# A six-layer cross network on one core: how the last layer's third round is evicted, and where the pending sum stands

## The chip, the core and the metric

The kernel runs on one core of a Trainium2 chip. The metric is the device time of one execution in microseconds (us), as the median of several runs; lower is better. The engines are named as the profile names them: PE is the matrix engine (PEld its weight loads), DVE the vector engine, ACT the scalar engine, POOL GpSimd, and SP the engine whose queue issues most DMAs here. A "q" behind a name (SPq, ACTq) is that engine's instruction queue.

## What is computed

x0 has 4096 rows of 416 numbers, ws six matrices of 416 by 416, bs six rows of 416; all in bf16.

```python
def reference(x0, ws, bs):
    x = x0
    for l in range(ws.shape[0]):
        x = x0 * (x @ ws[l] + bs[l]) + x
    return x
```

## The kernel before

**Layers 0 to 4** work on the transposed state: features lie on the partitions (three groups of 128 features in `XM`, the last 32 features packed for four column groups in `XR`), and the 4096 rows of the batch lie along the free dimension. PE multiplies with the layer's weights, ACT adds the bias while it copies the result out of PSUM to bf16 (L159), DVE multiplies by x0 (L160) and adds the old state (L161). While layer 4 ends, DMA transposes write its result back with rows on the partitions (`XLrows`, L197), since the output needs rows.

**The last layer** (from L292) exchanges the operands, so that its result has rows on the partitions: a block is 128 rows by 416 outputs. There are 32 blocks, worked off in four rounds of eight. A round covers two "quads" of four blocks. Per round four PSUM tiles are allocated, each with two banks, so that each of the eight blocks has a bank. The pool `psum` has four such tiles, so a tile of a round can be written only when the tile that held its place in the round before has been read by ACT. Which block has which bank is written in the lists `PAIRS`, `TURNS` and `ENDS` (L336 to L338): in `PAIRS` blocks 1 and 2 share a tile, then 3 and 4, and so on; in the other two lists neighbours mostly have different tiles.

PE's order in a round is that of the code at L348 to L354. First come the full products of the first `done` blocks (three matmuls of 128 by 416 each, L304), then for the first quad four matmuls with the last 32 features (L310) and four that add the bias by a row of ones (L313), then the same eight for the second quad, and then the full products of the remaining blocks, each of which closes its block. The last round has `done` = 1, the others 2. A step of PE is in order: a matmul that waits for its tile holds up all behind it.

**Eviction.** `close(u, n)` (L344) calls `ew` (L324) for n neighbouring blocks in one tile, one or two. `ew` lets ACT cast the block or pair from PSUM to bf16 (`t`, L331), DVE multiply it by x0 (`X0rows`, L332), and then calls `close_sum`, which issues what is pending from the block or pair before: DVE's sum with `XLrows` into `o` (L321) and the DMA of `o` to the output (L322). Then its own sum is put into `pending`. So DVE's order is product, sum of the one before, next product, and so on, and `keep_in_program_order` keeps this order. A sum is thus never directly behind its own product. The output DMAs are issued from SP's queue, that of the very last block from ACT's queue. The pool of `t` has 6 buffers, that of `o` has 10.

In the first two rounds blocks are evicted in pairs. In the third round the first two blocks are a pair and the other six are single; in the fourth all eight are single.

Of the kernel before, what the change touches and what calls it, by code (L numbers as in the profile page):

```python
# [16 lines left out]
def kernel(  # L17
# [7 lines left out]
    nc = tc.nc  # L25
    B, D = x0.shape
# [232 lines left out]
    for l in range(1, LL):  # L259
        nxt, nxtR = XM[1 + (l % 2)], XR[1 + (l % 2)]  # L260
        feeds_last = (l == LL - 1)
        tiles = [(s, m) for s in range(NS) for m in range(NK)]
# [31 lines left out]
    NQ = len(quads)  # L294
# [7 lines left out]
    def mm_q_full(q, g, py, closes):  # L302
        for k in range(NK):
            nc.tensor.matmul(py[:, 0:D], lhsT=cur[:, k, q_cols(q, g)], rhs=WM[:, l, k, :],  # L304
                             start=((not closes) and k == 0), stop=(closes and k == NK - 1))

    def mm_q_rem(q, py, done):
        s, i = quads[q]
        for g in range(NG):
            nc.tensor.matmul(py[g][:, 0:D], lhsT=curR[32 * g:32 * g + 32, CW * s + 128 * i:CW * s + 128 * i + 128],  # L310
                             rhs=WR[32 * g:32 * g + 32, l, :], start=(g >= done), stop=False, tile_position=(32 * g, 0))
        for g in range(NG):
            nc.tensor.matmul(py[g][:, 0:D], lhsT=ones[32 * g:32 * g + 1, :],  # L313
                             rhs=bLr[32 * g:32 * g + 1, :], start=False, stop=(g < done), tile_position=(32 * g, 0))
# [3 lines left out]
    def close_sum():  # L318
        while pending:
            o, t, xl, dst, eng = pending.pop()  # L320
            tc.keep_in_program_order(nc.vector.tensor_tensor(out=o, in0=t, in1=xl, op=ALU.add))  # L321
            eng.dma_start(dst, o)  # L322

    def ew(q, g0, n, src, eng):  # L324
        s, i = quads[q]
        b0 = 16 * s + 4 * g0 + i
        b = slice(b0, b0 + 4 * (n - 1) + 1, 4)
        t = tpool.tile([P, 2 * CW], BF16, name="t")
        o = opool.tile([P, 2, D], BF16, name="o")
        tv = t[:, 0:n * D].rearrange("p (a d) -> p a d", a=n)  # L330
        nc.scalar.copy(tv, src)  # L331
        tc.keep_in_program_order(nc.vector.tensor_tensor(out=tv, in0=tv, in1=X0rows[:, b, :], op=ALU.mult))  # L332
        close_sum()
        pending.append((o[:, 0:n, :], tv, XLrows[:, b, :], out_v[:, b, :], eng))

    PAIRS = [(0, 0), (0, 1), (1, 0), (1, 1), (2, 0), (2, 1), (3, 0), (3, 1)]  # L336
    TURNS = [(0, 0), (0, 1), (1, 0), (2, 0), (3, 0), (1, 1), (2, 1), (3, 1)]
    ENDS = [(0, 0), (1, 0), (2, 0), (0, 1), (3, 0), (1, 1), (2, 1), (3, 1)]  # L338
    rounds = [(0, PAIRS, 2), (2, PAIRS, 2), (4, TURNS, 2), (6, ENDS, 1)]
    for q, at, done in rounds:  # L340
        tiles = [psum.tile([P, 2, CW], FP32, tag="ps", name=f"py{n}") for n in range(4)]
        bank = [tiles[n][:, a, :] for n, a in at]

        def close(u, n):  # L344
            tl, a = at[u]
            ew(q + u // 4, u % 4, n, tiles[tl][:, a:a + n, 0:D], nc.scalar if q + 2 == NQ and u == 7 else nc.sync)

        for u in range(done):  # L348
            mm_q_full(q, u, bank[u], False)
        mm_q_rem(q, bank[0:4], done)  # L350
        close(0, done)
        mm_q_rem(q + 1, bank[4:8], 0)
        for u in range(done, 8):
            mm_q_full(q + u // 4, u % 4, bank[u], True)  # L354
            if at is not PAIRS:
                close(u, 1)
            elif u % 2:
                close(u - 1, 2)
# [31 lines left out]
```

## Time and profile before

| | us |
|---|---|
| median of 3 runs | 131.48 (131.47 to 131.52) |
| the profiled execution | 131.97 |
| its span, first to last instruction | 130.1 |
| PE busy | 124.2 (95%) |
| DVE busy | 107.5 (83%) |
| ACT busy | 85.8 (66%) |
| last layer's first full matmul starts | 104.84 |
| last full matmul ends | 125.6 |
| last cast ends | 126.14 |
| last sum starts | 127.01 |
| last output DMA issued (ACT's queue) | 127.42 |

The granted clock of PE was 0.999 over the span. The busy time of an engine counts the time in which at least one of its instructions runs. DVE instructions overlap: the next one starts before the one before it is shown as ended, so what an instruction costs on a busy DVE is the step from its start to the next start, not its duration. The end of a matmul is modelled. A timeline line gives the start, the duration, engine, line of the code, operation, output and inputs, the shapes, and how many were merged; in brackets stands how long the engine had been idle before it and what ended that. The chain of work that ended last, by engine, is PE 89%, DVE 6%, issue 2%, ACT 1%.

### The profile page before, as it was taken

How to read it: one execution, taken by the hardware profiler on the slowest of the kernel's cores; microseconds unless marked ns; L12 is line 12 of the kernel's file. 1: busy time of each engine (PE TensorE's matmuls, PEld its weight loads, DVE VectorE, ACT ScalarE, POOL GpSimd, SP SyncE). 2: the span in 40 equal slices, each digit the busy share in tenths (PEclk: the TensorE clock that was granted, in tenths of full speed). 3: DMA queues.
4: the chain of work that ended last, by engine and by line, in shares of the span. 5: the costliest groups of instructions: out<-in, count | busy, mean ns of one | idle time of the engine just before them, and what ended most of it. 6: DMA issues, size and time to landing. Idle time of an engine off the chain costs nothing.

```text
span 130.1 us, 3968 instructions
## 1 busy us (share of the span) xinstructions
PE 124.2 (95%) x1688; PEld 55.2 (42%) x1690; DVE 107.5 (83%) x197; ACT 85.8 (66%) x97; POOL 5.8 (4%) x17
## 2 busy tenths in 40 slices
PE   6999999999999999999999999999999999999960
PEld 2343343444444444545444434444445445445420
DVE  1012989999998898999898989898989899898991
ACT  0044594788849485849486849577848896569670
POOL 4002110610000000000000000000000000000000
PEclk9999999999999999999999999999999999999999
DMA  3999999999990000000000000000197999995754
GB/s 102 211 219 225 149 198 242 243 327 333 333 306 12 5 0 3 5 0 5 0 5 0 5 0 5 0 0 5 30 176 162 121 220 180 195 306 191 234 170 132
DMA packets 42185, 16.45 MB, mean 126 GB/s; under 512 B 30894, under 2 KB 42168, under 8 KB 42168
## 3 DMA queue, kind: packets, MB, share of 16 engines
q1 hardware_dynamic: 39368, 15.53, 54.4%
q10 hardware_dynamic: 2800, 0.67, 2.8%
q8 instruction: 13, 0.21, 0.7%
q14 instruction: 4, 0.03, 0.1%
HBM read 6.23 MB, written 3.41 MB: 74 GB/s over the span
## 4 chain that ended last, share of the span: by engine, by line
PE 89%; DVE 6%; issue 2%; ACT 1%; DVEq 0%
PE pt L173 49%; PE ph L208 13%; PE py L304 8%; PE pt L179 5%; PE pr L190 5%; DVE t L332 3%; PE wps L135 3%; DVE o L321 2%; PE pr L185 2%; PE ph L226 2%; PE py L310 1%; PE py L313 1%; ACT t L331 1%; PE tpr L151 0%; PE pr L151 0%
## 5 line engine op out<-in xcount | busy, mean ns | idle before, releaser
L173 PE MATMUL pt<-XM,WM 128*32 128x512 bf16 x1152 | 65.2, 379 | 0.0
L159 ACT ACTIVATE t<-pt,bM 128x1024 bf16<-128x1024 f32 x48 | 49.6, 1115 | 17.6 <-PE pt L179 17.6
L160 DVE TENSOR_TENSOR t<-t,XM 128x1024 bf16<-128x1024 bf16 x60 | 41.3, 690 | 6.0 <-ACT t L159 6.0
L161 DVE TENSOR_TENSOR XM<-t,XM 128x1024 bf16<-128x1024 bf16 x60 | 41.7, 696 | 3.4
L173 PEld LDWEIGHTS <-WM 128*32 128x32 bf16 x1152 | 29.8, 97 | 33.9 <-issue 5.4
L331 ACT CAST t<-py 128x416 bf16<-128x416 f32 (+1 forms) x23 | 14.8, 642 | 4.8 <-PE py L304 2.6
L304 PE MATMUL py<-WM,XM 128*128 128x416 bf16 x96 | 17.7, 340 | 0.0
L159 ACT ACTIVATE t<-ph,bM 128x1024 bf16<-128x1024 f32 x12 | 12.5, 1112 | 7.5 <-PE ph L226 7.5
L208 PE MATMUL ph<-XM,WM 128*128 128x512 bf16 x70 | 16.9, 387 | 0.2
L304 PEld LDWEIGHTS <-XM 128*128 128x128 bf16 x96 | 9.0, 98 | 8.5 <-issue 1.4
L332 DVE TENSOR_TENSOR t<-t,X0rows 128x416 bf16<-128x416 bf16 (+1 forms) x23 | 10.4, 456 | 1.2 <-ACT t L331 1.2
L208 PEld LDWEIGHTS <-WM 128*128 128x128 bf16 x72 | 6.9, 99 | 8.9 <-issue 1.9
L321 DVE TENSOR_TENSOR o<-t,XLrows 128x416 bf16<-128x416 bf16 (+1 forms) x23 | 10.4, 455 | 0.0
L165 ACT ACTIVATE t<-pr,bR 128x512 bf16<-128x512 f32 x10 | 6.4, 685 | 3.0 <-PE pr L190 2.1
L190 PE MATMUL pr<-XM,WM 128*32 128x512 bf16 x120 | 8.2, 379 | 0.0
L179 PE MATMUL pt<-XR,WR 32*128 32x512 bf16 x96 | 7.3, 379 | 0.0
L106 ACT ACT_TABLE_LOAD x1 | 1.3, 1283 | 6.6 <-DMA XM<-in_x_dram 6.6
L135 PE MATMUL wps<-warm 128*128 128x512 bf16 (+1 forms) x11 | 4.4, 593 | 1.2 <-DVE warm L94 1.2
L167 DVE TENSOR_TENSOR XR<-t,XR 128x512 bf16<-128x512 bf16 x10 | 4.2, 425 | 0.7
L190 PEld LDWEIGHTS <-WM 128*32 128x32 bf16 x120 | 3.2, 97 | 3.0
L166 DVE TENSOR_TENSOR t<-t,XR 128x512 bf16<-128x512 bf16 x10 | 4.2, 418 | 0.0
L125 POOL COPY WD<-WR 32x32 bf16<-32x32 bf16 (+1 forms) x8 | 3.4, 424 | 16.6 <-DMA WR<-in_ws_dram 16.3
(37 smaller groups left out, 29.7 us busy)
## 6 DMA issues: line engine op xcount, KB each, us to landing
X0rows<-in_x_dram SPq DMA_DIRECT2D x4, 832.0 KB, 11.6
out_dram<-o SPq DMA_DIRECT2D x9, 208.0 KB, 2.5
WM<-in_ws_dram SPq DMA_DIRECT2D x5, 312.0 KB
out_dram<-o SPq DMA_DIRECT2D x13, 104.0 KB, 1.8
WR<-in_ws_dram SPq DMA_DIRECT2D x4, 130.0 KB, 4.1
WM<-in_ws_dram ACTq DMA_DIRECT2D x1, 312.0 KB
XM<-in_x_dram SPq DMA_TRANSPOSE x8, 5.8
xrig<-in_x_dram ACTq DMA_DIRECT2D x4, 32.0 KB, 4.5
```

Of the source, the lines that this page charges most:

```text
L135: nc.tensor.matmul(wps[:, 0:cols], lhsT=warm[:, 0:P], rhs=warm[:, 0:cols], start=True, stop=True)
L159: nc.scalar.activation(t[:], pt[:].rearrange("p a b -> p (a b)"), ACT.Identity, bias=bM[:, m, l:l + 1], scale=1.0)
L160: nc.vector.tensor_tensor(out=t[:], in0=t[:], in1=XM[0][:, m, c0:c0 + 2 * CW], op=ALU.mult)
L161: nc.vector.tensor_tensor(out=nxt[:, m, c0:c0 + 2 * CW], in0=t[:], in1=cur[:, m, c0:c0 + 2 * CW], op=ALU.add)
L173: nc.tensor.matmul(pts[g // 2][32 * q:32 * q + 32, g % 2, :], lhsT=WM[:, l, k, 128 * m + 32 * q:128 * m + 32 * q + 32], rhs=cur[:, k, c0:c ...
L179: nc.tensor.matmul(pts[g // 2][:, g % 2, :], lhsT=WR[32 * g:32 * g + 32, l, 128 * m:128 * m + 128], rhs=curR[32 * g:32 * g + 32, CW * s:CW ...
L190: nc.tensor.matmul(pr[32 * g:32 * g + 32, :], lhsT=WM[:, l, k, NK * P:D], rhs=cur[:, k, c0:c0 + CW], start=False, stop=(k == NK - 1), tile ...
L208: nc.tensor.matmul(pt[m][:, gl, :], lhsT=WM[:, 0, k, 128 * m:128 * m + 128], rhs=cur[:, k, c0:c0 + CW], start=(k == 0), stop=False)
L304: nc.tensor.matmul(py[:, 0:D], lhsT=cur[:, k, q_cols(q, g)], rhs=WM[:, l, k, :], start=((not closes) and k == 0), stop=(closes and k == NK ...
L321: tc.keep_in_program_order(nc.vector.tensor_tensor(out=o, in0=t, in1=xl, op=ALU.add))
L331: nc.scalar.copy(tv, src)
L332: tc.keep_in_program_order(nc.vector.tensor_tensor(out=tv, in0=tv, in1=X0rows[:, b, :], op=ALU.mult))
```

## The change

The third round uses `PAIRS`: its eight blocks have their banks like those of the first two rounds, and are evicted as four pairs. `TURNS` is gone. And `ew` has a new argument `late`: where it is true, the pending sum is issued ahead of the pair's own cast and product, so that on DVE the sum of the pair before comes first and the product second. It is true for pairs in the second and third rounds that begin with the first or third block (u = 0 and u = 2); for the other pairs, the first round and the fourth round the order stays.

```diff
-    def ew(q, g0, n, src, eng):
+    def ew(q, g0, n, src, eng, late):
+        if late:
+            close_sum()
         s, i = quads[q]
...
     PAIRS = [(0, 0), (0, 1), (1, 0), (1, 1), (2, 0), (2, 1), (3, 0), (3, 1)]
-    TURNS = [(0, 0), (0, 1), (1, 0), (2, 0), (3, 0), (1, 1), (2, 1), (3, 1)]
     ENDS = [(0, 0), (1, 0), (2, 0), (0, 1), (3, 0), (1, 1), (2, 1), (3, 1)]
-    rounds = [(0, PAIRS, 2), (2, PAIRS, 2), (4, TURNS, 2), (6, ENDS, 1)]
+    rounds = [(0, PAIRS, 2), (2, PAIRS, 2), (4, PAIRS, 2), (6, ENDS, 1)]
...
-            ew(q + u // 4, u % 4, n, tiles[tl][:, a:a + n, 0:D], nc.scalar if q + 2 == NQ and u == 7 else nc.sync)
+            ew(q + u // 4, u % 4, n, tiles[tl][:, a:a + n, 0:D], nc.scalar if q + 2 == NQ and u == 7 else nc.sync,
+               q > 0 and n == 2 and u < 4)
```

With this DVE has 20 products and 20 sums in the last layer instead of 23 each, ACT 20 casts instead of 23, and there are 20 output DMAs instead of 23. PE has the same matmuls in the same order of blocks.

## Prediction

> **What bounds the kernel now.** I read the chain of work that ended last first (it stays on PE until 116.84 us and then runs on DVE), then the timeline of the last layer, instruction by instruction, then the waits. I call the eight blocks of a round 1 to 8, a product P (L332), a sum S (L321), so S78 is the sum of the pair 7 and 8. The timeline, third round (from 116.86 us) into the fourth; columns are start, duration, engine, line, operation, shapes, count:
>
> ```profile
> 116.23 0.59 DVE L332 TENSOR_TENSOR t<-t,X0rows 128x832 bf16<-128x832 bf16 x1
> 116.74 0.58 DVE L321 TENSOR_TENSOR o<-t,XLrows 128x832 bf16<-128x832 bf16 x1
> ...
> 117.75 0.59 DVE L332 TENSOR_TENSOR t<-t,X0rows 128x832 bf16<-128x832 bf16 x1 [0.43 <-ACT t L331]
> 118.26 0.59 DVE L321 TENSOR_TENSOR o<-t,XLrows 128x832 bf16<-128x832 bf16 x1
> 118.76 0.37 DVE L332 TENSOR_TENSOR t<-t,X0rows 128x416 bf16<-128x416 bf16 x1
> ...
> 121.28 0.34 PE L310 MATMUL py<-WR,XR 32*128 32x416 bf16 x4
> ...
> 122.40 0.37 DVE L332 TENSOR_TENSOR t<-t,X0rows 128x416 bf16<-128x416 bf16 x1
> 122.47 3.67 ACT L331 CAST t<-py 128x416 bf16<-128x416 f32 x7 [0.47 <-PE py L304]
> 122.69 0.37 DVE L321 TENSOR_TENSOR o<-t,XLrows 128x416 bf16<-128x416 bf16 x1
> 123.01 0.38 DVE L332 TENSOR_TENSOR t<-t,X0rows 128x416 bf16<-128x416 bf16 x1
> 123.31 0.37 DVE L321 TENSOR_TENSOR o<-t,XLrows 128x416 bf16<-128x416 bf16 x1
> ...
> 126.44 0.37 DVE L332 TENSOR_TENSOR t<-t,X0rows 128x416 bf16<-128x416 bf16 x1
> 126.73 0.66 DVE L321 TENSOR_TENSOR o<-t,XLrows 128x416 bf16<-128x416 bf16 x2
> 127.42 0.37 ACTq L322 DMA_DIRECT2D out_dram<-o  x1
> ```
>
> Three things are to be seen. First, steps from start to start on DVE: about 0.505 us behind a pair operation (116.23 to 116.74; 118.26 to 118.76) and 0.285 behind a single one (122.40 to 122.69). A block costs 0.57 in singles (P and S) and 0.505 in pairs. Second, the fourth round: block 2's cast begins at 122.47 and takes 0.51, so it ends at 122.98, and P2 starts at 123.01. DVE would have been free at 122.69 + 0.285 = 122.97. So at 123.01 DVE has just caught up with PE and ACT: it carries no arrears out of the third round. From there 14 steps of 0.286 lead without a gap to the last sum (127.01, the second of the x2), its DMA at 127.42 and the end. The arrears at the end are made in the fourth round, where a block takes DVE 0.57 and ACT 0.53. The last cast ends at 122.47 + 3.67 = 126.14, P8 starts at 126.44. Third, PE has nothing to give back: from 104.84 to 125.6 its matmuls run at their own step, and the waits name no engine that PE waits for in that stretch after its first load.
>
> So the end is the start of P2 in the fourth round plus fixed work, and the question is what the change does to that start.
>
> **The change, part by part.**
>
> *Third round in pairs.* Six blocks of casts, products and sums become three pairs. PE's number and order of matmuls stay; only the banks differ. ACT's four casts then repeat the second round's pattern, 0.85 each: there they start at 111.72, 113.24, 114.29 and 115.35, and the full matmuls at 111.97. In the third round the full matmuls start at 117.12, 5.15 later, which puts the casts at 116.86, 118.39, 119.44 and 120.49, the last until 121.34.
>
> *DVE in the third round*, by these casts, with 0.03 from the end of a cast to its product (117.72 to 117.75). P12 at 117.75 as before. S12 is now next and needs P12's end: 117.75 + 0.59 + 0.03 = 118.37. P34 waits for its cast: 119.27. P56 waits for its cast: 120.33; its pending S34 may not go first, as only the first two pairs of a round have the new order, so DVE sits idle for 0.55. S34 at 120.84. P78 waits: 121.38. S56 at 121.89. P1 of the fourth round at 121.89 + 0.50 = 122.39, against 122.40 before. Then S78, a pair where there was a single: it starts at 122.68 and P2 can start at 122.68 + 0.50 = 123.18. That is 0.17 later than 123.01; before, P2's step to its sum was 0.29 because it had waited, so 0.16 of it arrives at the end. The saving of the pairs (six blocks at 0.57 against 0.505, 0.39 us) is spent waiting for later, longer casts, and what is left over at the seam is a longer operation ahead of P2.
>
> *PE at the seam.* In the fourth round the fourth tile is written first by the L310 group at 121.28 (blocks 5 to 8). It must wait until the third round's last cast has read that tile: before, a single cast that ended at 121.00; now the pair's, at 121.34. All matmuls behind it wait too: the full products of blocks 2 to 8, and through them ACT's seven casts. The stall is 121.34 − 121.28 plus the way from ACT to PE. One place in the trace shows that way:
>
> ```profile
> 26.61 1.11 ACT L159 ACTIVATE t<-ph,bM 128x1024 bf16<-128x1024 f32 x1 [1.40 <-PE ph L226]
> 27.78 0.38 PE L173 MATMUL pt<-XM,WM 128*32 128x512 bf16 x1
> ```
>
> ACT ends at 27.73 and PE's waiting matmul starts at 27.78: 0.05. The other engine shows more: DVE's product at 103.90 ends at 104.59 and PE's load for it starts at 104.83, 0.24 later, part of which is PE's own change from the earlier layer. So the stall lies between 0.06 and 0.30; I take 0.11, by the row of the same pair of engines. Block 2's cast then ends at 122.98 + 0.11 = 123.09 and P2 could start at 123.12, ahead of 123.18: DVE's delay covers it. The two do not add; the later one counts. Without DVE's cover the stall would cost its 0.11.
>
> *The pending sum ahead of the product* at the first two pairs of the second and third rounds. Second round: S78 of the first round moves from 113.11 to 112.14, into an idle 0.38. P12 then starts at 112.65 instead of 112.60, S12 (behind its own product, 0.62) at 113.27, and DVE is free at 113.77, before P34's cast lets it go at 114.12. So this is worth nothing, hidden by the idle 0.42 before 114.12; without that cover it would cost 0.16. In the third round S78 fits from 117.25 to 117.75. Nothing on DVE waits there for XLrows: its last transpose had landed by 114.08.
>
> *DMAs.* SP's queue issues 19 output transfers instead of 22, three of them twice as large, and S78's earlier. The last transfer stays a single block on ACT's queue. The ten output buffers now turn over more slowly: the last sum waits for the landing of the pair 3 and 4 of the third round (sum ends at 121.4, median 2.5 to landing, so by 124), against a use at 127. Nothing.
>
> **Sum.** The profiled execution took 131.97 us with a span of 130.1; +0.16 gives 132.13. The runs' median is 131.48, 0.49 below the profiled one; the same +0.16 gives **131.64 us**, +0.12%. A measurement of this kernel can tell about 0.2% (0.26 us) from no change, so this counts as the same.
>
> [...]
>
> **Rivals.**
>
> *The saving arrives* (chance 0.06). If P2 were not pushed back and casts came as before, the 0.39 would go into the end, but only until DVE waits for the last cast: P8 cannot start before 126.14 + 0.03, so at most 126.44 − 126.17 = 0.27, and the time would be 131.21 to 131.22. For it: DVE is without a gap from 123.01 to the end. Against it: at 123.01 DVE met its cast, so work saved before that time cannot be carried past it. The Trainium skill's page "VectorE: DVE Perf Modes", section "Rules for kernel authors", tells to minimise the number of operations rather than semaphores, which would argue for this rival; the trace's wait at 123.01 speaks against it.
>
> *PE's stall decides* (chance 0.22, the slower side). The mechanism is the fourth tile at 121.28. If the release takes as long as DVE's row (0.24), the stall is 0.30, block 2's cast ends at 123.28, P2 starts at 123.31 and everything behind it is 0.30 late: 131.78, +0.23%. From a stall of 0.17 on it takes over from DVE; from 0.26 on it counts as slower. For it: one in-order queue, all remaining casts behind it. Against it: the 0.05 of the ACT row.
>
> *Nothing moves* (chance 0.10). The seam's S78 is hidden after all, by a P1 that comes earlier or by shorter steps, and the stall is at its lower end: 131.48 to 131.54. The program's order of instructions shows that the pairs and the moved sums are really there, so that the change doesn't do what it says is not left as a case.
>
> **How the numbers follow.** The forecast has 0.62: 131.64. Same: forecast and "nothing moves", 0.72. Slower by over 0.2%: the stall, 0.22. Faster by over 0.2%: 0.06, since at best 0.27 us is to be had. The range runs from no change to the stall at its upper bound with a little for the landing of the last transfer: 131.45 to 131.80.
>
> **What would show it.** In the profile after: casts of 0.85 at about 118.39, 119.44 and 120.49; DVE idle before P56 (about 0.5); S78 as a pair at 122.68 and P2 near 123.18; the L310 group near 121.39 instead of 121.28; the last DMA issue near 127.58. I am wrong if P2 starts before 123.05 (then work was carried over that I count as lost), if the L310 group starts after 121.45 (then the stall sets the end), or if the end moves without P2 (then it lies in the last landing).

## The result, and the profile after

The changed kernel took 132.53 us as the median of 6 runs (132.34 to 132.62), the kernel before beside it 131.47 (6 runs): a ratio of 1.0077, 95% interval 1.0067 to 1.0087. It is slower by 1.06 us. The prediction was 131.64, with a range up to 131.80.

The profiled execution after took 132.62 us, span 130.6. Executions differ in how long the first loads take: in the two profiles the last layer's first full matmul starts at 104.84 (before) and 104.39 (after). So I compare times counted from that matmul; a time of the profile after plus 0.45 is on the clock of the profile before.

DVE at the seam of the third and fourth round, timeline of the profile after (start, duration, engine, line, operation, shapes):

```profile
119.87 0.59 DVE L334 TENSOR_TENSOR t<-t,X0rows 128x832 bf16<-128x832 bf16 x1 [0.46 <-ACT t L333]
120.38 0.58 DVE L321 TENSOR_TENSOR o<-t,XLrows 128x832 bf16<-128x832 bf16 x1
120.92 0.59 DVE L334 TENSOR_TENSOR t<-t,X0rows 128x832 bf16<-128x832 bf16 x1
121.43 0.58 DVE L321 TENSOR_TENSOR o<-t,XLrows 128x832 bf16<-128x832 bf16 x1
121.94 0.37 DVE L334 TENSOR_TENSOR t<-t,X0rows 128x416 bf16<-128x416 bf16 x1
122.22 0.58 DVE L321 TENSOR_TENSOR o<-t,XLrows 128x832 bf16<-128x832 bf16 x1
122.72 0.37 DVE L334 TENSOR_TENSOR t<-t,X0rows 128x416 bf16<-128x416 bf16 x1
```

P56 waits for its cast with DVE idle for 0.46, S78 is a pair, and P2 of the fourth round starts at 122.72 + 0.45 = 123.17 (predicted 123.18). PE and the end of the last layer, same view:

```profile
120.46 0.35 PE L310 MATMUL py<-WR,XR 32*128 32x416 bf16 x4
120.94 0.36 PE L310 MATMUL py<-WR,XR 32*128 32x416 bf16 x4
...
126.15 0.36 DVE L334 TENSOR_TENSOR t<-t,X0rows 128x416 bf16<-128x416 bf16 x1
126.43 0.65 DVE L321 TENSOR_TENSOR o<-t,XLrows 128x416 bf16<-128x416 bf16 x2
126.52 0.81 SPq L322 DMA_DIRECT2D out_dram<-o  x2
127.12 0.37 ACTq L322 DMA_DIRECT2D out_dram<-o  x1
```

The L310 group that waits for the fourth tile starts at 120.94 + 0.45 = 121.39 (predicted 121.39, before 121.28), the last output DMA is issued at 127.12 + 0.45 = 127.57 (predicted 127.58, before 127.42). So the engines did what was forecast, and they explain 0.15 of 1.06 us. The rest lies behind the last instruction of any engine. The DMA issues on the page after (count, size, median us from issue to landing), then those of before. These medians hide more than they show:

```profile
out_dram<-o SPq DMA_DIRECT2D x12, 208.0 KB, 3.3
...
out_dram<-o SPq DMA_DIRECT2D x7, 104.0 KB, 2.4
```

```profile
out_dram<-o SPq DMA_DIRECT2D x9, 208.0 KB, 2.5
...
out_dram<-o SPq DMA_DIRECT2D x13, 104.0 KB, 1.8
```

The page knows the landing of only a few of these transfers; among the seven single ones after it is that of the 19th alone. In the trace's own landing times, counted back from the end, the 13th to 17th transfers after land 1.66 to 1.84 after their issue, no later than those of the fourth round before (1.65 to 1.92). Only the last three are late: 2.23, 2.45 and 2.48, against 1.70, 1.65 and 1.72 before. SP's own waits from 126 us on, after and then before (us in total, times, longest):

```profile
SPq L387 <- DMA out_dram<-o: 2.1, 1, 2.1
```

```profile
SPq L385 <- DMA out_dram<-o: 1.5, 4, 0.5
```

SP's first check waits for the 19th transfer in both kernels: before, four more come behind that one, and after, one. So the single long wait tells the order of the checks, and not yet that something is late. The trace's landing times say what kind of lateness it is. Each transfer's semaphore is raised 16 times, and I take each time as one of the 16 DMA engines. In the last three transfers after, 15 of the 16 came in 1.81, 1.73 and 1.88 us after the issue, the sixteenth 0.42, 0.71 and 0.61 later still; before, the sixteenth was 0.02 to 0.03 behind in the last three. Of the 0.76 that the very last transfer lost, 0.58 is this sixteenth part; the other 0.18 is that the fifteen came later too. This points at one DMA engine that was held up. On the queues that the page names "instruction", one packet lies in this stretch: on q14 a fetch of 8 KB begins at 125.75 before (0.55 us long) and at 127.67 after (0.61 us long, on the clock of before).

```profile
q8 instruction: 13, 0.21, 0.7%
q14 instruction: 4, 0.03, 0.1%
```

The whole queue is 0.1% of the DMA engines' span on the page after, and the same four fetches are on the page before. The page does not show where in time they lie. Up to this fetch SP has 82 rows in the trace before, and 82 after; DVE has 244 and 243, ACT 188 and 183. That SP's row count stays is the lead: it may be SP's instructions that are fetched. DVE's count moves by one only, so the decision lies with those runs below that change the number of SP's DMAs alone. In all profiles the other three fetches on q14 stay where they are on the clock of before (36.9 to 37.0, 51.3 to 51.5, 111.0 to 111.4); only the fourth moves with SP's DMAs.

The other instruction queue, q8, shows the same thing where no engine is seen to wait for it. A fetch of 16 KB begins there at 116.42 before and at 116.22 after, in the middle of the last layer; in the transfers then in flight the sixteenth landing lags by up to 1.92 and 1.91, and is level again (0.01) by the 12th transfer before and the 10th after. So a lag of one sixteenth behind an instruction fetch is not special to SP's queue; it matters when the kernel ends before it has worn off.

SP's own stream has a second sign. Its output DMAs show a pause at the same one of them in both kernels; after:

```profile
125.68 0.33 SPq L322 DMA_DIRECT2D out_dram<-o  x1
...
126.52 0.33 SPq L322 DMA_DIRECT2D out_dram<-o  x1
...
126.96 0.37 SPq L322 DMA_DIRECT2D out_dram<-o  x1
```

The issues before these follow each other at 0.57. The 18th, at 126.52, comes 0.84 after the 17th and 0.29 after its sum has ended (126.23); behind all others of the fourth round on SP's queue up to the 17th that is 0.03. In the profile before it is again the 18th, at 125.11, 0.29 after its sum's end. There, five transfers follow; after, two.

The account, from the last layer's first full matmul on, in us:

| | before | after | difference |
|---|---|---|---|
| last output DMA issued | 22.58 | 22.73 | +0.15 |
| from there to its last landing | 1.72 | 2.48 | +0.76 |
| from there until SP has checked all landings | 0.08 | 0.28 | +0.19 |
| from there to the end of the span | 0.93 | 0.75 | -0.18 |
| outside the span | 1.82 | 2.00 | +0.17 |
| sum | | | +1.09 |

The third row is the order of the checks. The output transfers use eight slots of DMA semaphores in turn, and SP ends by waiting for these slots in a fixed order, in five checks; where nothing is left to wait for, the checks are about 0.064 apart (the second to fifth start after at 129.616, 129.683, 129.747, 129.809). Before, the last transfer had the slot that is checked last. With three DMAs fewer it has one that is checked second, and three more checks follow its landing.

### The profile page after: what moved, and what is told of

Its sections match the earlier page's. It is cut to its first block, busy times and chain, and to the rows that moved or that the text cites. A ratio compares the mean times of both kernels' runs of the same rounds, so it can differ in the third digit from the quotient of the medians.

```text
span 130.6 us, 3949 instructions
## 1 busy us (share of the span) xinstructions
PE 124.0 (95%) x1690; PEld 55.2 (42%) x1690; DVE 107.2 (82%) x191; ACT 85.3 (65%) x94; POOL 6.1 (5%) x17
## 4 chain that ended last, share of the span: by engine, by line
PE 82%; SPq 5%; DMA 4%; DVE 4%; issue 2%; ACT 1%; DVEq 0%
PE pt L173 49%; PE py L304 9%; PE ph L208 9%; PE pt L179 5%; PE pr L190 5%; SPq L76 5%; DMA XM<-in_x_dram 4%; DVE t L334 3%; PE pr L185 2%; DVE o L321 1%; PE ph L226 1%; PE py L310 1%; PE py L313 1%; ACT t L333 1%; PE pr L151 0%
## 5 line engine op out<-in xcount | busy, mean ns | idle before, releaser
L161 DVE TENSOR_TENSOR XM<-t,XM 128x1024 bf16<-128x1024 bf16 x60 | 41.7, 696 | 3.4
L333 ACT CAST t<-py 128x832 bf16<-128x832 f32 (+1 forms) x20 | 14.3, 714 | 5.4 <-PE py L304 3.1
L334 DVE TENSOR_TENSOR t<-t,X0rows 128x832 bf16<-128x832 bf16 (+1 forms) x20 | 9.9, 499 | 1.5 <-ACT t L333 1.5
L321 DVE TENSOR_TENSOR o<-t,XLrows 128x832 bf16<-128x832 bf16 (+1 forms) x20 | 9.7, 497 | 0.1
```

The costliest lines, as they stand in the source:

```text
L161: nc.vector.tensor_tensor(out=nxt[:, m, c0:c0 + 2 * CW], in0=t[:], in1=cur[:, m, c0:c0 + 2 * CW], op=ALU.add)
```

## The experiments

All times are medians beside the kernel before on the same chip (131.52 or 131.53). The theory: three SP DMAs fewer move SP's instruction fetch from the 19th of 23 output transfers to the last. The second half, that they also move the last transfer to another place in the order of checks, was added after the first five runs. The rivals: A, the bytes (three transfers of 208 KB instead of six of 104 leave the queue behind); B, the moved sums (their transfers go out earlier into a crowded stretch); and later C, the fetch alone, and the pairs for the rest.

**Each half of the change alone.** pairs_only has the third round in pairs, and `ew` as before:

```diff
-    rounds = [(0, PAIRS, 2), (2, PAIRS, 2), (4, TURNS, 2), (6, ENDS, 1)]
+    rounds = [(0, PAIRS, 2), (2, PAIRS, 2), (4, PAIRS, 2), (6, ENDS, 1)]
```

> The third round in pairs, but every sum stays behind the next product. Theory (the position of SP's instruction fetch): three output DMAs fewer on SP, as in the changed kernel, so the 8 KB fetch again begins behind the 19th output DMA, which is now the last one on SP: 132.4 to 132.6 us, and the last transfer lands about 2.4 us after its issue. Rival A (bytes: three transfers of 208 KB leave the output queue behind): also 132.4 to 132.6. Rival B (the moved sums send transfers earlier into a crowded stretch, and the queue never recovers): 131.6, landing after 1.7.

Measured: 132.48 us, ratio 1.0067 (1.0053 to 1.0081). The fetch begins at 127.61, behind the last issue, and the last transfer lands 2.17 after its issue (about 2.4 was expected). late_only has the new `ew` with `TURNS` in the third round, so 23 output transfers.

> Only the order of the sums is changed; the third round keeps one pair and six single blocks, so 22 output DMAs on SP as before. Theory: the fetch comes behind the 19th of 22 as before, no change: 131.4 to 131.6 us. Rival A (bytes): the same. Rival B (moved sums): most of the loss, 132.2 or more.

Measured: 131.52 us, ratio 1.0003 (0.9995 to 1.0012); the fetch is at 125.75 as before, landing 1.72. The whole loss is with the pairs, and B falls: the moved sums do send transfers earlier, into the stretch behind the fetch on q8, but by the 14th the sixteenth landing is level with the others again (0.03). A and the theory stand.

**The last layer left alone, SP's DMAs ahead of it changed.** X0rows is loaded long before the last layer, which alone uses it. Its load is split differently, with the same bytes:

```diff
-    for q in range(4):
-        nc.sync.dma_start(X0rows[:, 8 * q:8 * q + 8, :], x0_v[:, 8 * q:8 * q + 8, :])
+    X0CUTS = [0, 4, 8, 12, 16, 20, 24, 26, 28, 30, 32]
+    for c0, c1 in zip(X0CUTS, X0CUTS[1:]):
+        nc.sync.dma_start(X0rows[:, c0:c1, :], x0_v[:, c0:c1, :])
```

In the labels, after or before is the kernel that is edited, and the number is that of the loads (X0CUTS of [0, 32] for one, [0, 8, 12, 16, 20, 24, 28, 32] for seven).

> The changed kernel, with the load of X0rows (needed only in the last layer) split into ten DMAs instead of four: six more SP DMAs long before the last layer, the same bytes. Theory: SP reaches the fetch three to six output DMAs sooner, the DMA engine that carries it recovers before the end: 131.55 to 131.75 us (only the 0.16 of DVE's seam is left), last landing 1.7 after its issue. Rivals A and B: 132.4 to 132.6 as the changed kernel, as the last layer is untouched.

Measured: 132.05 us, ratio 1.0043 (1.0028 to 1.0058). The fetch moved to 125.92, behind the 16th of 20, and the last landing came 1.80 after its issue. A falls: the last layer's bytes are the same as after, and the landing is back. But the time is 0.3 above the range expected.

> The kernel before, with X0rows loaded by one DMA instead of four: three SP DMAs fewer, the same bytes, the last layer untouched. Theory: the fetch moves one and a half to three output DMAs later, close to the last transfer: 131.8 to 132.4 us. Rivals A and B: 131.4 to 131.6.

Measured: 131.76 us, ratio 1.0020 (1.0010 to 1.0030). The fetch moved to 126.89, behind the 21st of 23, but the landing was only 0.11 longer, and the time is a little below the range expected. Most of its loss stands behind the landing: SP's checks took 0.27 instead of 0.08. Here the order of the checks was found: in this run the last transfer's slot is checked second, in after_x0_10 first (0.32 from landing to the end of checks).

**Fetch and checks apart.** Seven loads in the changed kernel move the fetch forward, and put the last transfer's slot last in the order, as it was before.

> The changed kernel with X0rows loaded by seven DMAs instead of four. In the earlier runs SP's fetch came at 82 to 83 of SP's rows in the trace, whatever was loaded; three more rows move it one and a half output DMAs sooner, behind the 17th or 18th of 20. And SP ends by checking the DMA semaphores of eight slots in a fixed order; the last transfer's slot is now the one that is checked last, as in the kernel before, while in the changed kernel three more checks of 0.064 follow it. Theory (fetch plus order of the checks): landing and checks back to normal, only DVE's 0.15 is left: 131.6 to 131.8 us. Rival C (fetch alone; the rest of the loss of the run with ten loads, 0.53 over the kernel before, is the cost of the pairs): 132.0, as with ten loads.

Measured: 131.70 us, ratio 1.0016 (1.0006 to 1.0027). SP's waits from 126 us on, with four short waits again, as the last transfer is checked last:

```profile
SPq L388 <- DMA out_dram<-o: 1.5, 4, 0.6
```

The landing is 1.82, the checks 0.08. Of 1.06 us 0.17 is left, with the same last layer as in the changed kernel, pairs, moved sums and all. C falls: the pairs cost no more than DVE's 0.15. The counterpart:

> The kernel before with X0rows loaded by seven DMAs. The fetch comes one and a half output DMAs sooner, where it recovers anyway; the last transfer's slot is now checked first, with four more checks behind it. Theory (fetch plus checks): 131.52 + 4 x 0.064 = 131.7 to 131.8 us. Rival C (fetch alone): 131.45 to 131.55.

Measured: 131.87 us, ratio 1.0023 (1.0013 to 1.0034; the medians differ by 0.34, the ratio says 0.30). SP's waits:

```profile
SPq L386 <- DMA out_dram<-o: 1.7, 1, 1.7
```

The fetch lies at 125.21, the landing is 1.75, the checks take 0.32: in the trace the order of checks costs 0.24, and the landing 0.03. The time is somewhat above the range expected.

> The changed kernel with X0rows loaded by one DMA. Three SP rows fewer put the fetch behind SP's last output DMA, with at most the one of ACT's queue still to land. Theory: SP's pause ahead of the 18th output DMA goes; if the fetch begins after the last transfer has been read out, landing is back to 1.7 and 131.8 to 132.0 us results (0.15 of DVE, three checks of 0.064 behind the last transfer); if it begins with it, 132.2 to 132.5. Rivals (bytes, moved sums): 132.5 as the changed kernel.

Measured: 131.98 us, ratio 1.0030 (1.0020 to 1.0039). SP's pause at the 18th output DMA is gone (issues at 126.14, 126.71, 127.28), the fetch begins at 128.82, 1.26 behind the last issue, the landing is 1.79, the checks take 0.26. A fetch that is late enough harms as little as an early one.

**The loss put into the kernel before.** The most direct test takes six SP DMAs away ahead of the last layer:

```diff
-    for g in range(NG):
-        nc.sync.dma_start(bLr[32 * g:32 * g + 1, :], bs[LL:LL + 1, :])
+    nc.sync.dma_start(bLr[0:P:32, :], bs[LL:LL + 1, :].broadcast_to([NG, D]))
```

> The kernel before with six SP DMAs fewer ahead of the last layer (X0rows by one DMA instead of four, the four copies of the last bias by one). Theory: the fetch moves three output DMAs later, behind the 21st or 22nd of 23, as near to the end as in the changed kernel; the last transfer's landing is late by 0.3 to 0.8 and three more checks follow it: 131.9 to 132.5 us, with a last layer that is untouched. Rivals (bytes, moved sums, pairs): 131.45 to 131.55.

Measured: 132.21 us, ratio 1.0051 (1.0037 to 1.0065). The 21st output DMA now has the pause (126.84, 0.86 behind the 20th), the fetch begins at 127.61, behind the last of all 23 issues (expected was the 21st or 22nd), the sixteenth landings of the last three transfers come 0.31, 0.44 and 0.31 behind the others, and SP waits once, as the last transfer's slot is checked second:

```profile
SPq L385 <- DMA out_dram<-o: 1.9, 1, 1.9
```

A kernel whose last layer is that of before lost 0.68 us (131.53 to 132.21) when loads ahead of it were issued in six DMAs fewer.

| run | output transfers | fetch begins behind | issue to last landing | landing to end of checks | median |
|---|---|---|---|---|---|
| before | 23 | 19th | 1.72 | 0.08 | 131.47 |
| late_only | 23 | 19th | 1.72 | 0.08 | 131.52 |
| before_x0_7 | 23 | 18th | 1.75 | 0.32 | 131.87 |
| before_x0_1 | 23 | 21st | 1.83 | 0.27 | 131.76 |
| before_m6 | 23 | 23rd | 2.21 | 0.25 | 132.21 |
| after | 20 | 20th | 2.48 | 0.28 | 132.53 |
| pairs_only | 20 | 20th | 2.17 | 0.27 | 132.48 |
| after_x0_10 | 20 | 16th | 1.80 | 0.32 | 132.05 |
| after_x0_7 | 20 | 18th | 1.82 | 0.08 | 131.70 |
| after_x0_1 | 20 | 20th, 1.26 later | 1.79 | 0.26 | 131.98 |

In all profiles of this study SP has 81 to 83 rows up to this fetch, DVE 235 to 249, ACT 182 to 189.

**The seam on DVE.** What is left of the loss was put down to S34, which stands behind P56, which waits for its cast. So the sum goes first at all pairs:

```diff
-               q > 0 and n == 2 and u < 4)
+               q > 0 and n == 2)
```

> The changed kernel with seven X0rows loads (the run that came to 131.70 us), and the pending sum ahead of the product at all pairs of the second and third rounds, not only the first two. Theory of the seam (a sum that waits behind a product that waits for its cast leaves DVE idle for half a us before the third pair of the third round): the idle time is used, P2 of the fourth round is no longer held up by DVE but by PE's stall on the fourth tile, and starts 0.10 to 0.12 behind the kernel before instead of 0.16; the last sum 0.10 behind: 131.60 to 131.70 us. If the pairs themselves were too slow for DVE, the last sum would stay 0.16 behind.

Measured: 131.85 us, ratio 1.0019 (1.0009 to 1.0028). That is above the range expected; its runs spread from 131.53 to 131.98, so as a time it tells nothing of 0.03 us. Its timeline does (0.49 to be added for the clock of before):

```profile
118.78 0.59 DVE L335 TENSOR_TENSOR t<-t,X0rows 128x832 bf16<-128x832 bf16 x1 [0.30 <-ACT t L334]
119.41 0.59 DVE L322 TENSOR_TENSOR o<-t,XLrows 128x832 bf16<-128x832 bf16 x1
119.92 0.58 DVE L335 TENSOR_TENSOR t<-t,X0rows 128x832 bf16<-128x832 bf16 x1
...
122.65 0.38 DVE L335 TENSOR_TENSOR t<-t,X0rows 128x416 bf16<-128x416 bf16 x1 [0.22 <-ACT t L334]
```

S34 (119.41) fills the time in which P56 would wait, and P2 (122.65) is no longer behind DVE: DVE is idle for 0.22 and the cast releases it, at 123.14 on the clock of before. That is 0.13 behind 123.01, and the last sum is 0.13 behind too (0.10 to 0.12 expected): PE's stall, which DVE had covered, shows. The stall is 0.11 at the L310 group, as in the changed kernel, and block 2's cast, which it holds up, ends 0.13 later than before (123.11 against 122.98). Both parts of the seam are there about as predicted.

**A version that might beat both.** The kernel before ends with DVE 0.26 behind the casts. One sum of the last round on POOL would take a step of 0.285 from DVE:

```diff
+                        nc.gpsimd if q == 6 and g0 == 3 else nc.vector))
```

(the adder is kept with the pending sum and used in `close_sum`).

> The kernel before, with the sum of the fourth block of the last round on POOL instead of DVE. Theory (the end of the kernel before is DVE's arrears of 0.26 against the casts, made in the last round): DVE has one step of 0.285 less, the product of the last block starts at its cast's end, the last sum 0.26 sooner: 131.25 to 131.35 us, if POOL's sum is done by about 126 and does not slow DVE; SP's transfers queue behind it meanwhile. If POOL takes longer or slows DVE: 131.5 or more.

Measured: 132.03 us, ratio 1.0042 (1.0028 to 1.0056). POOL's row and DVE's in the same stretch:

```profile
124.23 0.98 POOL L321 TENSOR_TENSOR o<-t,XLrows 128x416 bf16<-128x416 bf16 x1 [98.23 <-DMA out_dram<-o]
...
124.00 0.37 DVE L321 TENSOR_TENSOR o<-t,XLrows 128x416 bf16<-128x416 bf16 x1
124.29 1.43 DVE L332 TENSOR_TENSOR t<-t,X0rows 128x416 bf16<-128x416 bf16 x2
```

POOL's sum takes 0.98, and DVE's product that starts while it runs takes 1.15 instead of 0.37 (the two products, merged, 1.43); it ends 0.24 after POOL's sum. The last sum starts 0.50 later than before. The Trainium skill's page "Perfetto Trace Analysis", section "Optimizing Scalar/DVE Operations", warns that the two engines share a read port, so that moving work between them might not help; here it cost more than it moved. No version that beats the kernel before was found.

## Why the prediction was wrong

*What bounds the kernel.* Right as far as the last issue: the end is P2 of the fourth round plus fixed work. Wrong in "fixed": the way from the last issue to the end was taken as constant. It came to 1.72 + 0.08 before and 2.48 + 0.28 after.

*Third round on DVE.* Right: P2 at 123.18, measured 123.17; the delay at the last sum predicted 0.16, measured 0.16. The run with seven loads, where the landing and the checks are as before, has a median 0.17 above the kernel before.

*PE at the seam.* Right: stall predicted 0.11, measured 0.11 (121.28 to 121.39), covered by DVE; late_all_x0_7 uncovered it. The row at 103.90 that the prediction sets beside it as DVE's product is the sum of L161; the bound of 0.24 read from it stays. The rival "PE's stall decides" was wrong, with its condition (0.17) not met. The result fell on its side of the bound, by another cause.

*The pending sum ahead of the product.* Right: worth nothing, 131.52 against 131.52 alone.

*DMAs.* This is the step that failed. It read: "SP's queue issues 19 output transfers instead of 22 [...] The last transfer stays a single block on ACT's queue. [...] Nothing." It priced what is transferred, and not the instructions that issue it. Three DMAs fewer on SP moved its instruction fetch by two us, onto the last three transfers (+0.76), and the last transfer to an earlier place in the order of checks (+0.19). The signs of the fetch were in the trace of before: its packet at 125.75, the sixteenth landings that lag behind it by up to 0.20 and have caught up by the last, the pause at the 18th issue. How much it would cost further back could not be read there. The prediction does not name the fetch or the checks; nothing waited for the fetch in the kernel before.

*What would show it wrong.* "if the end moves without P2 (then it lies in the last landing)" named the sign, but no rival and no chance stood for it; the range left 0.02 for the landing (131.80 over the stall's 131.78).

*What stays open.* The last two rows of the account (-0.18 and +0.17) cancel; the span's tail was shorter in every profile with 20 casts (0.75 against 0.93 to 0.94), and the part outside the span was longer in each of these kernels (on the mean of its runs 1.93 to 2.03, against 1.79 to 1.82 with 23). Why was not tried. That the lagging sixteenth DMA engine is the one that carries the fetch is inferred from time, not read: the trace's packets do not tell their engine. What makes SP pause ahead of the fetch is open too; pause and fetch moved together in the runs, so the part of each in the fifteen landings that came 0.18 later is not told apart. And the size of the landing's delay is not explained. With the same order of issues it is 0.45 in pairs_only and 0.76 after, where the fetches took 0.47 and 0.61; but before_m6 lost 0.49 by a fetch of 0.31, so the fetch's length does not settle it.

## What to carry to other kernels

When an edit takes instructions off a queue that issues DMAs, look for the instruction fetch in that queue's stream and count rows to see where it falls next; near the end nothing covers it, and a pure loss of 0.5% (before_m6) can come from work that got less. Compare how far the last landing lies behind its issue, and how far its sixteenth part lies behind the other fifteen, before blaming the engines' work. A test that splits or merges an unrelated early load shifts the fetch without touching the part under study, and tells an effect of position from an effect of the change. It also shifts the last transfer's place in the order of the checks, which has to be read beside it.

## What the runs showed of the hardware

- The fetch on q14 that moves with the number of SP's DMAs is 8 KB and took 0.31 to 0.63 us in the twelve profiles; the transfers around it had one of their 16 landings up to 0.71 us behind the others (after). That it takes this time on one of the DMA engines that carry the data is inferred. The Trainium skill's page "Runtime: NRT & Kernel Launch", section "Instruction fetch mechanics", has refills of 16 KiB and their cost as mostly hidden. The fetches of the other instruction queue, q8, were 16 KB here. The cost of SP's was hidden behind the 19th of 23 output transfers; 0.10 behind the last issue it was not, +0.76 us, and 1.26 behind the last issue (after_x0_1) it was again nearly hidden, the landing at 1.79 instead of 1.72.
- SP paused for about 0.26 us ahead of the 18th output DMA in both kernels, and ahead of the 21st with six DMAs fewer; the fetch began 0.64, 0.70 and 0.77 us after these issues.
- The place of the last transfer in the order of SP's final checks was worth 0.24 us in the trace: 0.32 from landing to the end of checks where it is checked first (before_x0_7), 0.08 where it is checked last (before). That run took 131.87 against 131.53; its fetch had moved by one transfer too, with the landing 0.03 later.
- While a sum of 0.98 us ran on POOL, DVE's product that started in it took 1.15 us instead of 0.37 (before_pool3).
